# Attention with beacon keys and a low-rank mixer: values of the first batch loaded in long rows and held until the first q is there, first pair turned in two parts

## The chip, the cores and the metric

The kernel runs on one core of a Trainium2 chip. A core has engines that work side by side, each on its own list of instructions in order: TensorE (PE: matmuls and transposes, with PEld for its weight loads), VectorE (DVE), ScalarE (ACT), GpSimd (POOL) and SyncE (SP). Transfers are issued from the lists of SP, ACT and POOL. The metric is the time of one execution in microseconds on the device.

## The reference

Eight batches, eight heads, 576 tokens, head size 64. Sixteen "beacon" keys and values stand ahead of each head's 576; they are seen by all tokens. The attention's output, with the heads side by side (512 wide), goes through a mixer of rank 32 over the tokens and then through an MLP 512 to 2048 to 512 with a residual.

```python
k_all = concatenate([beacon_k, k], axis=2)          # 16 + 576
v_all = concatenate([beacon_v, v], axis=2)
scores = q @ k_all.T / sqrt(64)                     # causal, beacons always seen
a = softmax(scores)
x = (a @ v_all).transpose(0, 2, 1, 3).reshape(8, 576, 512)
u = x + (x.transpose(0, 2, 1) @ U @ V).transpose(0, 2, 1)
out = u + maximum(u @ w_ch1, 0) @ w_ch2
```

## The kernel before

**Tiles.** Two heads make a pair; there are 32, four to a batch. For each pair k and q are turned (head size on partitions), scores are computed transposed (keys on partitions) in four visits a to d for both heads, each visit followed by two exponentials on ACT out of PSUM into `expt`. DVE masks by a minimum, PE multiplies with the values (`po`), DVE divides by the sum that a column of ones gives, into `xb`. When a batch's four pairs are done the mixer forms `uT`, a ring of three blocks of 512 tokens. The MLP runs over nine such blocks: 16 products `g` a block for the hidden layer, then seven products of a two-by-two scheme with sums on DVE (`p`, `W`, `P`).

**The order.** `SCRIPT` is a list of steps, written out; every engine's list is in the script's order. A step's name gives engine and pair where it matters: V is DVE, A is ACT, G is POOL. `GkV1` casts or regroups pair 1's k on DVE (`regroup`, L294). `HqA0` casts pair 0's short q rows ("heads", the first 64 or 80 rows, `first_heads`, L791) on ACT. `TkA1` turns pair 1's k on PE and copies it out on ACT (`qkT_units`, L302 to L308). `Sb2:1` is visit b of pair 2 with one filler matmul (`keep_warm`, L282); `I1` is one filler alone. `M0.1` and `A0.1` are mask and value product of pair 0, head 1. `X0.0` to `X0.2` are the mixer of batch 0, whose last two write `uT`. `g0.5` is a hidden product of block 0, `R12` a turn of a pair by a transfer. `k1A`, `q1B`, `v0A`, `b1` and `w10` are loads, with A and B the halves of four heads.

**The first batch.** Its q and k come in f32 over SP's and ACT's lists (`load_first`), pair by pair, into `stm` (512 main rows) and `sth` (heads). All other loads are issued by POOL and cast to f16 on the way. A main row of q or k is four tokens in a row of DRAM, 1,024 bytes of f32.

**Values.** `v_loads` (L212) fetches them in five loads for a half batch, one token and head (64 numbers) a piece, straight into `vs`, where partitions are tokens. For a batch in `PACKED`, `packed_loads` (L220) fetches 448 of the 576 tokens four at a time into a tile `xt` and the rest as before; the step `O` (`unpack`, L231) then brings them to `vs` by 16 matmuls with a 0/1 matrix `unp` (filled by the step `n`) and four copies out of PSUM, two on DVE and two on ACT. Before, only batch 1 is packed.

**Buffers.** PSUM tiles come from one pool of eight buffers in turn, so a matmul waits until the tile eight before is copied out. `hold`, the step `Y` (L793), lets POOL copy one number of a loaded tile; what stands behind it on POOL is issued only when that tile has landed. No step `Y` stood in the script before.

Of the kernel before, what the change touches and what calls it, by code (L numbers as in the profile page):

```python
# [27 lines left out]
def kernel(  # L28
# [267 lines left out]
    def qkT_units(L, pr, qT, kT, c, copies):  # L296

        hs = ds(2 * c, 2)

        def one(i, dst, w):  # L300
            ps = pst([P, SK], F16, name="tps")
            nc.tensor.transpose(ps[:, 0:NL], L[0][i][:NL, hs, :], ident[:NL, :NL])  # L302
            for j in range(4):
                nc.tensor.transpose(ps[:, ds(NL + P * j, P)], pr[:, i, j, :, :], ident)  # L304
            copies[i](out=dst[:, c, 0 : w - 4 * P], in_=ps[:, 0 : w - 4 * P])
            copies[i](
                out=dst[:, c, w - 4 * P : w].rearrange("x (p j) -> x p j", j=4),
                in_=ps[:, NL:SK].rearrange("x (j p) -> x p j", j=4),  # L308
            )
# [529 lines left out]
    def step(t):  # L839
# [75 lines left out]
        v1B b2 M5.0 g0.8 GqV7 GqV6 TkA6 TkA7 M4.1 g0.10 M4.0 U0.1 TqA7 w13 TqA6 A5.0 GqA9 A5.1 GqV8 A4.1
        A4.0 Sd7 Sc7 g0.2 Sd6 Sc6 Sb6 g0.7 g0.3 k2 O1B g0.6 GqV10 Sb7 Sa6:0 Sa7 p00.0 w20 M6.0 g0.12 g0.13
        p00.1 GkV8 w21 v2 M7.1 GkV9 GkA10 g0.15 M7.0 TqA8 A6.0 TqA10 M6.1 p00.2 TkA9 A7.0 A7.1 TkA8 TqV9
        A6.1 g0.14 g0.4 Sb8 Sc8 Sd8 X1.0 p01.0 TkV10 P01.0 X1.2 Sa8 GqV11 p01.1 P01.1 GkV11 b3 X1.1 W0 Sb9
        P02.0 Sd9 Sc9 Sa9 W4 W1 W5 M8.0 W2 W6 TqA11 M8.1 TkA11 b4 P02.1 U1.1 M9.1 p01.2 M9.0 P05.0 U0.3
        P05.1 P06.0 q3 P06.1 A9.1 k3 A8.1 A8.0 W3 A9.0 P03.0 q4 P03.1 Sb11 Sa11 g1.10 GqV14 GqV13 k4 g1.7  # L920
        g1.2 GkA13 P07.0 Sb10 Sc11 Sd11 GkA12 GkV14 g1.15 g1.1 GqV12 g1.3 R12 M11.0 R13 R14 g1.12 g1.9 g1.8
        g1.14 g1.4 Sc10 Sd10 Sa10 W7 M11.1 P07.1 M10.1 b5 g1.5 U1.0 A11.1 g1.6 U1.3 A10.1 TkV13 TkV12 TqA13
        g1.0 P04.0 g1.13 M10.0 v3 TqV12 GqV16 P04.1 A10.0 GkV15 g1.11 GkV17 p11.0 TkV14 A11.0 p10.0 U1.2
        Sb12 Sc12 Sc13 P11.0 P11.1 GqA15 R15 X2.0 p11.1 Sa12 Sd12 Sa13 p10.1 M12.1 P16.0 p10.2 M12.0 X2.1
        p11.2 TqA14 q5 P12.0 P12.1 GkV16 A12.0 GqA17 R16 A12.1 P16.1 U2.2 P15.0 R17 Sd13 Sb13 Sc14 x12
        P15.1 TkV15 P17.0 P17.1 Z16 M13.1 Sa14 Sd14 TqA15 Sb14 U2.3 P13.0 M13.0 P13.1 GkA19 g2.11 TkA16
        M14.1 A13.1 v4 A13.0 P14.0 M14.0 TqA16 P14.1 Sa15 Sb15 Sd15 A14.0 GqV19 A14.1 g2.14 Sc15 Sb16 Sc16
        GkV18 M15.0 M15.1 GqV20 TqV17 g2.2 TkA17 g2.13 A15.0 A15.1 g2.9 N5 g2.0 x14 Sd16 Sa17 Sd17 g2.7
        g2.6 X2.2 X3.0 Sb17 Sc17 N1 Sa16 x13 g2.8 k5 M17.0 GqV18 U2.0 M16.0 g2.3 x15 M17.1 g2.10 b6 R18 R19
        U2.1 g2.1 g2.15 GkV20 M16.1 A16.0 A17.1 X3.2 R20 Z18 q6 g2.4 b7 p20.0 g2.5 p20.1 g2.12 A16.1 GkA21  # L930
        P21.0 p21.0 X3.1 P21.1 TkA18 P22.0 TqA18 GqV21 GkV22 TqA19 P22.1 p21.1 TkA19 A17.0 p21.2 Sb18 Sc18
        p20.2 P26.0 P26.1 GkV23 Sd18 k6 GqV22 Sa19 Sa18 M18.0 P25.0 P25.1 M18.1 P27.0 GqA23 Sb19 Sd19 Sc19
        TqA20 P23.0 R21 U3.0 M19.0 M19.1 P27.1 x16 GqA24 P23.1 TkA20 TqV21 v5 g3.1 g3.11 A18.1 g3.9 R22
        A19.0 A19.1 TkV21 g3.3 g3.14 g3.13 Sd21 Sb21 Sc21 R23 P24.0 g3.12 A18.0 q7 g3.5 P24.1 Sb20 U3.3
        U3.1 Sd20 g3.10 Sa21 Sa20 Sc20 X4.0 g3.6 GkV24 M21.0 M21.1 g3.8 M20.0 g3.7 TkA22 M20.1 TqV23 g3.15
        g3.2 x17 g3.4 GkV25 g3.0 A21.1 R24 x18 p31.0 TkA23 p31.2 A21.0 P31.0 Sa23 Sc23 Sb23 TqA22 p30.0
        GqA25 U3.2 P31.1 P32.0 A20.0 A20.1 p30.2 x19 R25 P32.1 GqA26 Sd23 Sc22 P36.0 GkV26 Sa22 Sb22 Sd22
        p30.1 GkV27 p31.1 GqA28 R26 M23.1 TkV24 GqA29 GqA27 k7 M22.0 P36.1 P35.0 X4.1 TqA25 A23.1 P35.1
        P37.0 P37.1 X4.2 A22.0 TqA24 U4.1 P33.0 TkA26 P33.1 g4.1 M23.0 v6 GkA29 GkA28 g4.2 M22.1 g4.12 R27
        N6 N2 TqA26 g4.7 g4.11 R28 g4.3 g4.14 TkA25 g4.15 A22.1 Sc24 Sa24 A23.0 g4.10 P34.0 v7 Sb25 Sb24  # L940
        Sd24 g4.5 R29 g4.6 P34.1 TqV27 Sc25 Sa25 Sd25 M24.1 M25.0 M25.1 TkA27 g4.4 g4.8 g4.13 M24.0 U4.3
        A25.0 g4.0 A25.1 Sd27 Sc27 Sb27 X5.0 p41.0 A24.0 x21 p41.1 g4.9 A24.1 Sa27 Sa26 Sc26 p40.0 M27.0
        P41.0 p40.1 GqV31 P42.0 A27.0 M27.1 U4.2 GkA30 U4.0 x22 Sb26 p41.2 GkV31 x23 Sd26 p40.2 P45.0 M26.1
        P45.1 x20 A27.1 P41.1 P42.1 TqA29 TkV28 M26.0 TqA28 P43.0 X5.1 GqA30 U5.3 R30 P46.0 A26.1 P46.1
        P43.1 g5.12 U5.1 x27 g5.4 TkV29 g5.2 g5.5 N3 N7 g5.0 Sa29 Sd29 Sc29 P47.0 P47.1 A26.0 Sb29 Sd28
        M29.0 M29.1 Sb28 P44.0 g5.3 g5.1 R31 x24 A29.0 P44.1 X5.2 g5.6 g5.15 Sa28 Sc28 TqV31 A29.1 TqV30
        TkV31 M28.0 x25 g5.7 U5.0 N4 g5.10 M28.1 TkV30 g5.9 Sa31 Sb31 Sd31 A28.0 g5.8 A28.1 g5.11 X6.0 Sd30
        x29 x26 Sc31 X6.1 V6.0 g5.14 p50.0 M31.1 p50.1 g5.13 p51.0 p51.1 Sa30 Sb30 Sc30 P51.0 M31.0 A31.1
        M30.1 P51.1 P55.0 M30.0 x28 P52.0 A31.0 A30.1 p50.2 U5.2 P56.0 U6.1 A30.0 p51.2 V6.1 P56.1 x31
        P55.1 P52.1 X7.0 X6.2 P57.0 x30 N0 P57.1 F61.0 P53.0 X7.1 V6.2 P53.1 U6.2 P54.0 F66.0 X7.2 F65.0  # L950
        F61.1 F62.0 F67.0 F62.1 P54.1 U7.2 F63.0 F61.2 F65.1 F66.1 V6.3 F65.3 F62.2 F61.3 F65.2 F67.1 F62.3
        V7.2 U7.0 U7.3 F64.0 V7.0 F66.2 U7.1 F63.1 V7.1 U6.3 F66.3 F63.2 F75.0 F71.3 F71.0 F64.1 F67.3
        F76.3 p60.0 F67.2 F63.3 p61.0 F64.3 P61.0 p60.1 F64.2 F75.3 p61.1 p60.2 V8.0 U6.0 P61.1 P62.0 P65.0
        P65.1 V7.3 F76.0 P66.0 p61.2 P62.1 P63.0 P66.1 P63.1 F72.3 F77.3 F77.0 F75.2 F72.0 F75.1 F73.3
        F73.0 F71.2 P67.0 F71.1 F74.3 F72.2 F76.1 V8.2 F76.2 F81.0 F72.1 P67.1 F77.1 F77.2 F73.2 P64.0
        P64.1 p71.0 U8.2 F74.0 p71.1 F73.1 F74.1 P71.0 F81.1 p70.0 F85.3 p70.1 F74.2 P71.1 P72.0 P72.1
        P76.0 V8.1 P75.0 p71.2 p70.2 P75.1 P76.1 guard F86.1 V8.3 P73.0 F86.0 P73.1 F85.1 U8.1 P77.0 P77.1
        F82.0 F85.0 F82.1 F87.1 F87.0 F83.0 F83.1 F81.2 U8.0 F84.1 P74.0 F81.3 P74.1 p80.0 F86.2 F82.3
        p80.1 F86.3 F82.2 F85.2 F84.0 F87.2 F87.3 F83.2 F83.3 sum p81.0 F84.2 F84.3 P81.0 P81.1 U8.3 p81.1
# [122 lines left out]
```

## Time and profile before

| | us |
|---|---|
| median of three timed executions | 338.77 |
| the three | 339.65, 336.57, 338.77 |
| the profiled execution's own time | 336.31 |
| its span, first to last instruction | 334.6 |

The profile shows one execution, with the TensorE clock granted at 0.999 of full speed. Its span leaves out 1.7 us that lie around it. A row of the timeline gives the start, the time from the first start to the last end, the engine, the line, the operation with what it writes and reads, and a count. An instruction's time overlaps with that of the one behind it on the same engine, so spacings of starts are shorter than the durations. Square brackets tell how long the engine stood idle in front and what ended it. The chain of waits gives start, length and work, with no overlap.

Some rows that set the scene, from the timeline: what PE does until the first pair is in, and where it waits in the first 30 us.

```profile
1.58 4.88 PE L282 MATMUL idle<-ident 128*128 128x512 f16 x11 [1.58 <-POOL ident masks.py:199]
...
8.21 0.68 PE L357 MATMUL sps<-qT,kT 64*128 64x336 f16 x10 [0.35 <-DVE small L158]
...
15.48 1.21 PE L357 MATMUL sps<-qT,kT 64*128 64x208 f16 x10 [0.40 <-ACT kT L109]
...
23.69 0.63 PE L372 MATMUL po<-vs,expt 128*128 128x65 f16 x15 [0.61 <-DVE expt L345]
```

### The profile page before, as it was taken

To read this page: it belongs to the slowest core of one execution; us is meant where nothing else is said; L and a number is where in the kernel's file an instruction comes from. 1 tells how busy PE (TensorE), PEld (TensorE's weight loads), DVE (VectorE), ACT (ScalarE), POOL (GpSimd) and SP (SyncE) were. 2 spreads that over 40 slices of the span, in tenths; PEclk is the share of its full clock that TensorE was granted. 3 is DMA by queue.
4 is the path that set the end of the run, shared out by engine and by line. 5 is a ranking of instruction groups with operands and counts; after the bars stand their busy time and mean duration, and the time that the engine had idled before them with its cause. 6 is when DMAs were issued, how large, how long until landed. Compare 5 with 4: busy or idle time off the path is not lost.

```text
span 334.6 us, 8971 instructions
## 1 busy us (share of the span) xinstructions
PE 324.8 (97%) x3537; PEld 227.2 (68%) x3537; DVE 257.8 (77%) x684; ACT 232.0 (69%) x510; POOL 96.6 (29%) x125
## 2 busy tenths in 40 slices
...
GB/s 186 222 201 167 156 198 193 119 189 213 118 164 162 203 149 143 143 131 177 191 121 143 183 168 112 31 169 123 68 41 80 141 19 63 3 80 94 80 37 99
DMA packets 133393, 44.18 MB, mean 132 GB/s; under 512 B 104768, under 2 KB 129216, under 8 KB 133344
## 3 DMA queue, kind: packets, MB, share of 16 engines
...
q14 instruction: 20, 0.16, 0.2%
...
## 4 chain that ended last, share of the span: by engine, by line
PE 87%; DVE 5%; ACT 4%; DMA 2%; issue 1%; SPq 0%
PE gps L570 25%; PE cpY L661 19%; PE cpD L661 9%; PE sps L357 8%; PE po L372 7%; PE fpY L607 6%; PE cpA L661 4%; PE fpD L607 3%; ACT expt L362 3%; PE fpA L607 2%; DMA stm<-in_k_dram 1%; PE ups L438 1%; PE ups L431 1%; PE qtp L412 1%; PE tps L304 1%; DVE ob L686 1%
## 5 line engine op out<-in xcount | busy, mean ns | idle before, releaser
L362 ACT ACTIVATE expt<-sps 128x496 f16<-128x496 f32 (+2 forms) x256 | 110.5, 576 | 13.3 <-PE sps L357 7.5
L570 PE MATMUL gps<-uT,w 128*128 128x512 f16 x384 | 90.2, 379 | 0.2 <-DVE xb L381 0.2
L570 PEld LDWEIGHTS <-w 128*128 128x128 f16 x384 | 34.9, 98 | 39.5 <-issue 2.6
L661 PEld LDWEIGHTS <-gT 128*128 128x128 f16 x576 | 54.7, 98 | 9.4 <-issue 1.5
L628 POOL TENSOR_SCALAR gT<-gT 128x512 f16<-128x512 f16 x12 | 18.3, 1534 | 103.9 <-DVE gT L622 70.9
L661 PEld LDWEIGHTS <-sT 128*128 128x128 f16 x432 | 40.7, 98 | 6.9 <-issue 0.7
L575 DVE SCALAR_TENSOR_TENSOR gT<-gps,gT 128x256 f16<-128x256 f32 x48 | 19.7, 420 | 29.7 <-ACT gT L574 29.5
L372 PEld LDWEIGHTS <-expt 128*128 128x128 f16 (+1 forms) x960 | 34.4, 98 | 7.2 <-issue 1.3
L580 ACT ACTIVATE gT<-gps 128x512 f16<-128x512 f32 x48 | 29.9, 637 | 12.7 <-PE gps L570 12.7
L372 PE MATMUL po<-vs,expt 128*128 128x65 f16 (+1 forms) x960 | 37.1, 194 | 0.6 <-DVE expt L345 0.6
L661 PE MATMUL cpD<-w,sT 128*128 128x256 f16 x288 | 36.1, 273 | 0.0
L661 PE MATMUL cpY<-wsum,gT 128*128 128x256 f16 x288 | 36.1, 273 | 0.0
L357 PE MATMUL sps<-qT,kT 64*128 64x80 f16 (+4 forms) x384 | 34.0, 281 | 1.5 <-ACT kT L109 0.4
L381 DVE TENSOR_TENSOR xb<-po,rec 128x320 f16<-128x320 f32 x64 | 31.5, 491 | 2.2
L212 POOL DMA_DIRECT2D vs<-in_v_dram x40 | 32.6, 833 | 0.8 <-DMA hd<-in_k_dram 0.8
L109 ACT ACTIVATE hP<-fpY 128x512 f32<-128x512 f32 x24 | 14.0, 596 | 26.8 <-PE fpY L607 16.6
L345 DVE TENSOR_TENSOR expt<-expt,bigmask 128x512 f16<-128x512 f16 x64 | 26.7, 417 | 6.6 <-ACT expt L362 6.6
L574 ACT ACTIVATE gT<-gps 128x256 f16<-128x256 f32 x48 | 19.8, 440 | 12.3 <-PE gps L570 12.2
L357 PEld LDWEIGHTS <-kT 64*128 64x128 f16 x384 | 14.8, 94 | 19.2 <-issue 11.0
L686 DVE TENSOR_TENSOR ob<-cpY,ut 128x512 f32<-128x512 f32 (+1 forms) x28 | 18.6, 665 | 2.6 <-PE cpY L661 2.4
L607 PEld LDWEIGHTS <-wf 128*128 128x128 f16 x192 | 18.6, 98 | 2.6 <-DVE tb L549 0.2
L661 PE MATMUL cpY<-w,gT 128*128 128x256 f16 x144 | 18.4, 273 | 0.0
(123 smaller groups left out, 480.8 us busy)
## 6 DMA issues: line engine op xcount, KB each, us to landing
...
```

The source lines that it names most:

```text
L212: nc.gpsimd.dma_start(out=dst[a : a + nq[j], j, :, :], in_=src[hs, ds(q0[j], nq[j]), :].rearrange("h p d -> p h d"))
L345: nc.vector.tensor_tensor(out=e4, in0=e4, in1=bigmask, op=ALU.min)
L357: nc.tensor.matmul(ps[i][:, ds(o, w)], kT[hp, c, ds(P * ch, P)], qT[hp, c, ds(qa, w)], start=True, stop=True,)
L362: nc.scalar.activation(out=ex[i][:, ds(PAD + SLOT * g, gw[g])], in_=ps[i][:, 0 : gw[g]], func=AF.Exp, scale=scale)
L372: nc.tensor.matmul(po[:, j, :], ex[0 : nk[c], ds(blk[(c, j)], P)], vs[0 : nk[c], ds(c * H * E + h * E, E)], start=(c == 0), stop=(c == j),)
L381: nc.vector.tensor_tensor(out=xb[:, h // 2, :, ds(D * (h % 2), D)], in0=po[:, :, 0:D], in1=r.broadcast_to([P, NT, D]), op=ALU.mult)
L570: nc.tensor.matmul(g, w1[:, cc, ts(dc, P)], uT[:, cc, ds(ring(t0), 512)], start=(cc == 0), stop=(cc == NCC - 1))
L574: nc.scalar.activation(out=gT[:, dc, 0:H2], in_=g[:, 0:H2], func=AF.Relu)
L580: nc.scalar.activation(out=gT[:, dc, :], in_=g, func=AF.Relu)
L607: nc.tensor.matmul(ps[:, i, :], a[:, kk, ts(2 * mp + i, P)], b[:, kk, :], start=opens and i == 0 and kk == 0, stop=kk == 1, skip_group_che ...
L661: nc.tensor.matmul(ps[:, i, :], a[:, f, ds(P * i, P)], b[:, f, :], start=opens and i == 0 and f == 0, stop=f == NK - 1, skip_group_check=True,
L686: nc.vector.tensor_tensor(out=out, in0=ps[:, ii, :], in1=other, op=ALU.add)
```

## The change

Batch 0 is packed too, so its values come in eight loads instead of twelve and need two unpacks, `O0A` and `O0B`. A step `Yq0` stands in the script ahead of all loads on POOL: it holds them until the main rows of pair 0's q have landed. A new function turns a pair's main rows and its heads as two steps, `j` and `l`, each with a PSUM tile of its own; pair 0 uses them. And the script of some 940 steps is another, but for its last 324 (from `Sd27` on): which engine casts and copies what, the place of the loads, of `O1A` (now ahead of the mixer of batch 0) and of the later steps. Seven steps `I1` are gone.

```diff
-    PACKED = (1,)
+    PACKED = (0, 1)
...
+    def turn_part(L, pr, dst, c, i, main, copy):
+        w = (SK, S)[i]
+        ps = pst([P, SK], F16, name="tps")
+        if main:
+            for j in range(4):
+                nc.tensor.transpose(ps[:, ds(P * j, P)], pr[:, i, j, :, :], ident)
+            copy(
+                out=dst[:, c, w - 4 * P : w].rearrange("x (p j) -> x p j", j=4),
+                in_=ps[:, 0 : 4 * P].rearrange("x (j p) -> x p j", j=4),
+            )
+        else:
+            nc.tensor.transpose(ps[:, 0:NL], L[0][i][:NL, ds(2 * c, 2), :], ident[:NL, :NL])
+            copy(out=dst[:, c, 0 : w - 4 * P], in_=ps[:, 0 : w - 4 * P])
...
+        elif name in "jl":
+            b, c = divmod(int(arg[2:]), NH2)
+            i = "kq".index(arg[0])
+            turn_part(Ls[b], prs[int(arg[2:])], (kTs[b % 2], qT_of(b))[i], c, i, name == "j", COPY[arg[1]])
...
-        I1 GqV0 I1 HkA0 I1 I1 B GkA0 I1 I1 I1 v0A GkV1 v0B I1 I1 HqA0 I1 I1 TkA0 TqV0 TkA1 u Sc0 Sd0 Sb0
...
+        Yq0 I1 I1 HqA0 GkV0 I1 n v0A I1 u v0B I1 q1A q1B s I1 I1 GqV0 b1 I1 jkV0 HkV0 jqV0 lkA0 lqA0 B k1A
+        w10 GkV1 GqV1 Sb0 Sc0 TkV1 Sa0:3 TqV1 v1A GkV2 Sd0 Sd1 Sc1 M0.0 Sa1:2 M0.1 GqV2 O0A Sb1 w12 GkV3
...
```

POOL's list at its start, before: the value loads of both halves, then the first loads of batch 1 (`vs` are the values, `st` and `hd` main rows and heads of q and k).

```order
L759 MEMSET vs_128 128x40
L202 DMA vs_127<-in_beacon_v_dram 16x4x64
L212 DMA vs_127<-in_v_dram 112x4x64
L212 DMA vs_127<-in_v_dram 128x4x64 x3
L212 DMA vs_127<-in_v_dram 80x4x64
L202 DMA vs_127<-in_beacon_v_dram 16x4x64
L212 DMA vs_127<-in_v_dram 112x4x64
L212 DMA vs_127<-in_v_dram 128x4x64 x3
L212 DMA vs_127<-in_v_dram 80x4x64
L205 DMA st_296<-in_k_dram 128x4x256
```

The same place now, with the hold (`gate`) in front and `xt` as the tile of packed rows.

```order
L774 MEMSET vs_128 128x40
L810 COPY gate<-stm 1x1
L222 DMA xt<-in_v_dram 112x4x256
L202 DMA vs_127<-in_beacon_v_dram 16x4x64
L227 DMA vs_127<-in_v_dram 112x4x64
L227 DMA vs_127<-in_v_dram 16x4x64
L222 DMA xt<-in_v_dram 112x4x256
L202 DMA vs_127<-in_beacon_v_dram 16x4x64
L227 DMA vs_127<-in_v_dram 112x4x64
L227 DMA vs_127<-in_v_dram 16x4x64
L205 DMA st_209<-in_q_dram 128x4x256
```

Every load of POOL now stands behind the copy of one number of `stm`; behind the values comes batch 1's q, where its k came.

DVE's list behind its memsets, before: the first row is pair 0's q.

```order
L294 CAST pr<-stm 128x512
L118 MEMSET bigmask 128x16
L119 COPY bigmask<-mask 128x112
L121 COPY bigmask<-mask 128x128 x3
L294 CAST pr<-stm 128x512
L791 CAST hd_142<-sth 80x128
L305 COPY qT<-tps 128x64
L306 COPY qT<-tps 128x512
L158 MEMSET small 16x32
L294 CAST pr<-stm 128x512
```

And now: the second cast is pair 0's k, and the two copies at L320 are its turned main rows and q's.

```order
L294 CAST pr<-stm 128x512
L126 MEMSET unp 128x66
L127 TENSOR_REDUCE unp<-ident 128x32
L158 MEMSET small 16x32
L168 COPY one<-ident 32x32 x4
L294 CAST pr<-stm 128x512
L320 COPY kT_125<-tps 128x512
L806 CAST hd_142<-sth 80x128
L320 COPY qT<-tps 128x512
L118 MEMSET bigmask 128x16
L119 COPY bigmask<-mask 128x112
L121 COPY bigmask<-mask 128x128 x3
```

The fills of `unp` and `one` have moved up from behind pair 1, `bigmask` has moved back, pair 1's k is cast behind all of this, and pair 0's k is cast and copied here and no longer on ACT.

ACT's list at the later visits of pair 1 (`sps` are visits), before:

```order
L362 ACTIVATE expt_123<-sps_317 128x496
L362 ACTIVATE expt_124<-sps_318 128x496
L362 ACTIVATE expt_123<-sps_327 128x464
L362 ACTIVATE expt_124<-sps_328 128x464
L109 ACTIVATE kT_125<-tps 128x80
L109 ACTIVATE kT_125<-tps 128x512
L109 ACTIVATE kT_125<-tps 128x80
L109 ACTIVATE kT_125<-tps 128x512
```

The same place now (`vps` are unpacked values):

```order
L377 ACTIVATE expt_123<-sps_320 128x496
L377 ACTIVATE expt_124<-sps_321 128x496
L377 ACTIVATE expt_123<-sps_332 128x496
L377 ACTIVATE expt_124<-sps_333 128x496
L109 ACTIVATE vs_127<-vps 128x4x64
L109 ACTIVATE vs_127<-vps 64x4x64
L377 ACTIVATE expt_123<-sps_368 128x464
L377 ACTIVATE expt_124<-sps_369 128x464
L109 ACTIVATE kT_125<-tps 128x80
L109 ACTIVATE kT_125<-tps 128x512
```

The first unpack's two copies stand between visits a and b of pair 1, and one of the two turned k behind them has gone to DVE.

More of the change, by code (lines that the diff above doesn't have):

```diff
@@ L915 @@
[L915 to L959, printed above, removed]
@@ new lines @@
+        Sc12 Sb12 Sd13 GqV15 GkV15 TkA14 P11.1 P12.0 GqV16 P12.1 q5 R15 Sd12 TqA14 X2.0 Sa12 Sb13 Sc13
+        p11.2 GqV17 M12.1 GkA16 M12.0 P15.0 P16.0 p10.2 X2.1 P16.1 A12.1 R16 P15.1 U2.2 A12.0 P17.0 Sa13
+        Sd14 Sb14 M13.0 R17 M13.1 TkA16 P17.1 TqV15 TkV15 P13.0 x12 U2.3 P13.1 A13.1 GkV18 g2.9 A13.0 Sc14
+        Sa14 Sd15 P14.0 TqV16 M14.1 g2.1 g2.7 TkA17 Z16 Sa15 Sc15 Sb15 M14.0 P14.1 A14.0 v4 A14.1 g2.10
+        TqV17 M15.0 k5 x14 GkV19 b6 g2.5 GqV20 M15.1 Sc16 Sa16 Sb16 A15.0 g2.0 g2.2 A15.1 g2.8 X2.2 GqV18
@@ new lines @@
+        Sd16 X3.0 Sd17 M16.0 x13 U2.0 Sc17 Sb17 Sa17 A16.0 x15 GqA19 g2.6 M17.0 g2.15 g2.4 M16.1 g2.3 g2.11
+        g2.12 R18 P21.0 p20.0 p20.1 X3.2 GkV20 g2.13 R19 g2.14 U2.1 M17.1 A16.1 p21.0 GqV21 Z18 TkA18 X3.1
+        q6 A17.0 p21.1 GqV22 R20 P21.1 A17.1 TqA18 p20.2 TkA19 b7 P22.0 TqA19 P22.1 GkA21 R21 Sb18 GkV22
+        Sc19 P25.0 U3.0 p21.2 P26.0 k6 P26.1 Sb19 Sd19 Sa18 x16 P25.1 P27.0 P27.1 Sc18 Sa19 Sd18 P23.0 v5
+        P23.1 M19.0 TqA20 g3.4 g3.10 g3.15 M19.1 TkV21 TqV21 M18.1 g3.0 A19.0 R22 g3.1 GkV23 g3.2 A19.1
@@ new lines @@
+        A18.1 g3.6 GkA26 M18.0 g3.5 GqV23 Sa21 Sb21 g3.14 TkV20 A18.0 R23 g3.3 P24.0 Sd21 Sc21 Sd20 GqV26
+        P24.1 U3.3 M21.0 TqV22 GkV25 q7 g3.7 Sc20 Sb20 Sa20 TkV22 N1 g3.13 g3.9 M21.1 g3.11 U3.1 GkA24
+        M20.0 TkV23 g3.12 x17 TqV23 A21.0 A20.0 M20.1 GqA24 R24 p31.0 g3.8 A21.1 GqV25 Sc23 Sa23 Sb23 A20.1
+        x18 P31.0 p30.0 P31.1 Sd23 Sd22 X4.0 Sa22 U3.2 x19 p30.1 GkA27 p31.1 Sc22 Sb22 M23.0 p31.2 M23.1
+        R25 R26 P32.0 P36.0 P32.1 TkV24 TqA24 P35.0 p30.2 k7 P36.1 M22.0 X4.1 TkA25 GqA27 P35.1 P37.0 X4.2
@@ new lines @@
+        x20 A27.1 P41.1 P42.1 TqA29 TkV28 M26.0 TqA28 P43.0 X5.1 GqA30 U5.3 R30 P46.0 A26.1 P46.1 P43.1
+        g5.12 U5.1 x27 g5.4 TkV29 g5.2 g5.5 N3 N7 g5.0 Sa29 Sd29 Sc29 P47.0 P47.1 A26.0 Sb29 Sd28 M29.0
+        M29.1 Sb28 P44.0 g5.3 g5.1 R31 x24 A29.0 P44.1 X5.2 g5.6 g5.15 Sa28 Sc28 TqV31 A29.1 TqV30 TkV31
+        M28.0 x25 g5.7 U5.0 N4 g5.10 M28.1 TkV30 g5.9 Sa31 Sb31 Sd31 A28.0 g5.8 A28.1 g5.11 X6.0 Sd30 x29
+        x26 Sc31 X6.1 V6.0 g5.14 p50.0 M31.1 p50.1 g5.13 p51.0 p51.1 Sa30 Sb30 Sc30 P51.0 M31.0 A31.1 M30.1
```

34 lines of the change are left out of this document (29 added, 5 removed).

## The prediction

> **What bounds the kernel now.** I read the page's first lines, then the windows, the chain of waits, and last the timeline of each engine up to 35 us.
>
> ```profile
> span 334.6 us, 8971 instructions
> PE 324.8 (97%) x3537; PEld 227.2 (68%) x3537; DVE 257.8 (77%) x684; ACT 232.0 (69%) x510; POOL 96.6 (29%) x125
> ```
>
> ```profile
> core 0: us, PE busy (x) PEld busy (x) DVE busy (x) ACT busy (x) POOL busy (x), PEclk, DMA share, GB/s
> 10.00:15.00 5.00, 4.25 (x66) 2.76 (x64) 4.61 (x20) 5.00 (x13) 4.18 (x7) 1.00 1.66 217
> 20.00:25.00 5.00, 3.96 (x81) 3.00 (x77) 4.87 (x20) 5.00 (x15) 2.35 (x4) 1.00 1.35 201
> 25.00:30.00 5.00, 4.79 (x79) 2.84 (x76) 3.52 (x12) 3.94 (x11) 1.24 (x2) 1.00 1.49 192
> ...
> 30.40:55.00 24.60, 24.60 (x308) 13.93 (x311) 17.38 (x58) 24.16 (x65) 14.20 (x19) 1.00 1.50 175
> 55.00:72.00 17.00, 16.81 (x227) 12.83 (x228) 16.18 (x41) 10.73 (x28) 6.84 (x9) 1.00 2.32 153
> ```
>
> PE idles 9.8 us in all (334.6 less 324.8). The windows put its losses before 30 us: there ACT is busy without a break and DVE almost, and PE waits for both. From 30.4 us on PE is full. So the change, which alters every engine's work before 30 us, can win only there; an order after that can lose but hardly win.
>
> ```profile
> 8.63 6.18 ACT expt L362 x14
> 29.43 0.99 PE sps L357 x13
> 30.42 2.69 PE gps L570 x12
> 35.34 0.55 PE vps L240 x16
> 36.86 0.04 PE tps L302
> 36.90 0.22 PE tps L304 x4
> 52.65 1.73 PE gps L570 x8
> ```
>
> The chain has ACT's exponentials from 8.63 and PE's MLP products from 30.42. Those two marks frame the stage, so I work out where each lands after the change.
>
> **When the first exponential starts.** These are DVE's rows to 30 us that start after an idle time, and those that price its steps.
>
> ```profile
> 4.62 0.43 DVE L294 CAST pr<-stm 128x512 f16<-128x512 f32 x1 [2.97 <-DMA stm<-in_q_dram]
> 6.80 0.43 DVE L294 CAST pr<-stm 128x512 f16<-128x512 f32 x1 [1.30 <-DMA stm<-in_k_dram]
> 7.38 0.68 DVE L306 COPY qT<-tps 128x512 f16<-128x512 f16 x1
> 8.75 0.22 DVE L791 CAST hd<-sth 80x128 f16<-80x128 f32 x1 [0.27 <-DMA sth<-in_q_dram]
> 10.36 0.19 DVE L305 COPY qT<-tps 128x64 f16<-128x64 f16 x1 [1.38 <-PE tps L304]
> 11.06 0.42 DVE L294 CAST pr<-stm 128x512 f16<-128x512 f32 x1
> 11.39 0.41 DVE L791 CAST hd<-sth 80x128 f16<-80x128 f32 x1
> 12.01 0.57 DVE L168 COPY one<-ident 32x32 f16<-32x32 f16 x4
> 12.32 0.41 DVE L345 TENSOR_TENSOR expt<-expt,bigmask 128x512 f16<-128x512 f16 x1
> 16.55 0.42 DVE L345 TENSOR_TENSOR expt<-expt,bigmask 128x512 f16<-128x512 f16 x1 [0.37 <-ACT expt L362]
> 17.49 0.11 DVE L126 MEMSET unp<- 128x66 uint32 x1
> 17.64 0.38 DVE L127 TENSOR_REDUCE unp<-ident 128x32 f16<-128x128 f16 x1
> 27.84 0.72 DVE L447 CAST uT<-ups 128x240 f16<-128x240 f32 x2 [0.53 <-PE ups L438]
> 29.49 0.92 DVE L447 CAST uT<-ups 128x336 f16<-128x336 f32 x2 [0.93 <-PE ups L438]
> 36.37 0.75 DVE L244 CAST vs<-vps 128x256 f16<-128x256 f32 x2
> ```
>
> ```profile
> 5.70 0.61 ACT L109 ACTIVATE pr<-stm 128x512 f16<-128x512 f32 x1
> 6.22 0.29 ACT L109 ACTIVATE hd<-sth 80x128 f16<-80x128 f32 x1
> 6.88 0.72 ACT L109 ACTIVATE kT<-tps 128x80 f16<-128x80 f16 x2 [0.37 <-PE tps L304]
> ...
> 26.12 2.43 ACT L362 ACTIVATE expt<-sps 128x208 f16<-128x208 f32 x6 [0.68 <-PE sps L357]
> ...
> 29.45 0.79 ACT L449 ACTIVATE uT<-ups 128x336 f16<-128x336 f32 x2 [0.38 <-PE ups L438]
> 30.13 2.97 ACT L362 ACTIVATE expt<-sps 128x496 f16<-128x496 f32 x6
> 35.99 0.73 ACT L109 ACTIVATE vs<-vps 128x256 f16<-128x256 f32 x2
> ```
>
> Pair 0's q lands as before: DVE casts it at 4.62, and no value load competes with it in either order before then. The cast holds DVE 0.33 (11.06 to 11.39): 4.95. Then `unp` is filled, 0.53 (17.49 to 18.02): 5.48; four copies for `sel`, 0.31 (12.01 to 12.32): 5.8. k0's cast, which ACT began at 5.70, now follows on DVE: 6.13. From the end of that cast on ACT (6.31) to the copy of the turned rows (6.88) went 0.57, so the new main copy of k starts at 6.7; two such copies at 0.68 with a small head cast of 0.2 between end at 8.26. Before, the corresponding copy ended at 8.06 and the first exponential came 0.56 later. The new one is due at about 8.8, or 8.6 if the copies overlap their tails as before. I take 8.7: turning heads apart saves nothing, because DVE's list in front is full. Freeing the transfers from the value packets cannot help this mark, as k0 had landed before 5.70 already.
>
> **ACT to the last `uT` copy before the MLP.** Before: 8.63 to 30.13 is 21.5 us, less its idle 0.68 and 0.38 is 20.45 of work. Exponentials are the same 38, the turned copies for pairs 2 to 5 stay four. New are three unpacks (two for batch 0, and batch 1's first, now placed ahead of this mark) at 0.73, 2.2 us, and one head cast of 0.25 to 0.29 with q3. Sum 22.9; 8.7 and 22.9 make 31.6.
>
> **DVE to the same mark.** Before: 4.62 to 30.41, 25.8 us, less its idle (1.30, 0.27, 1.38, 0.37, 0.53, 0.93: 4.78) is 21.0. New: six casts of values (0.75 a pair), 2.25; seven full turned copies and two main ones for six full, 0.70 (10.36 to 11.06) and 1.36; two regroups more, at most 0.33 each. That is 5.0, so 26.0 and, begun at 4.62, 30.6 without any idle. The 0.57 behind k0's cast and about half of the last two waits remain, which makes 31.2 to 32.1. I take 31.6 for both engines.
>
> **PE.** The two added unpacks cost 2 x 0.55, the seven `idle` matmuls taken out are fillers; both lie in time in which PE waits, so they count nothing. That cover is PE's idle, 0.75 us between 10 and 15 and 1.04 between 20 and 25 in the windows above; were it gone, 1.1 us would show. The first MLP product moves from 30.42 to 31.6, 1.2 later. By then PE has done 0.55 (batch 1's unpack) and 0.26 (the turned q of pair 7) that came later before, and has still to do one visit of pair 4, 6 of 14 in 0.99, 0.42. So it is 1.2 - 0.39 = 0.8 us behind.
>
> **Loads.** The value loads wait for q0 on POOL, and all loads behind them too. The first row is POOL's first load in the timeline; the others are loads of the first 80 us in the view of transfers, with KB each and the us from issue to landing (unpacked values, then packed main rows).
>
> ```profile
> 2.30 0.72 POOL L202 DMA_DIRECT2D vs<-in_beacon_v_dram  x1
> ```
>
> ```profile
> vs<-in_v_dram POOLq DMA_DIRECT2D x6, 64.0 KB, 5.8
> ...
> xt<-in_v_dram POOLq DMA_DIRECT2D x2, 224.0 KB, 10.2
> ```
>
> Eight issues from about 4.8 at 0.72 end near 10.6, twelve from 2.30 near 10.9; what is queued behind keeps its time. Half A is wanted by its unpack at about 13. Bounds for its landing are 5.8 to 10.2 after the issue, 10.6 to 15.0; I take 12, nearest to the early loads, for 0 on the path. After 8.75 no idle time of DVE or ACT in the rows above ends with a transfer, so cheaper packets are worth 0. SP's queue keeps its order and stays free.
>
> **From 31 us on.** Engines, regroups and turned copies are dealt out anew up to about 225 us, in PE's full stage; I count 0. At most about 0.2 us of PE idle can be won there (17.00 less 16.81).
>
> [...]
>
> **Sum.** 336.31 (profiled execution) + 0.8 = 337.1. The four known executions run 336.31 to 339.65 with mean 337.8, and the median of the three timed is 2.46 above the profiled one. On the mean's scale the time is 338.6.
>
> **Rivals.**
>
> A, faster: DVE's waits at 6.80 to 10.36 (2.95) vanish and nothing takes their place, so both lists end at 30.6 to 30.9 with k0 turned early; then the first product is 0.2 to 0.4 late, less 0.39, and if the first exponential also starts 0.9 earlier, -0.9: 336.9. For it: those idle times are real. Against: ACT's 22.9 us cannot shrink. More than 1% (3.4 us) would take a third of all the idle time that PE has in the program.
>
> B, slower: the held values land late. If they land at 15.0, PE, which works in order, stands at the unpack, whose 0.55 end at 15.6. In front of it stand 14 exponentials, as in the chain's first row, some narrower: 8.7 and 6.18 make 14.9 at most, 14.4 with the narrow ones. ACT loses 1.0, for +1.8: 339.6. It decides from a landing at 14.1; for more than 1% slower it must land near 17. Against: the fewer packets. [...]
>
> C, slower: DVE becomes the bound between 55 and 72 us. It has 0.8 us of room (16.18 of 17.00), and between 31 and 57 us three turned copies and two regroups more are dealt to it, 2.6 us, which eat into its 7.2 us of room in 30.4 to 55. If none of that is worked off by 55, PE waits up to 2.6 for DVE there: with the forecast's 0.8, +3.4 at the far end, +1.8 if half of it stays: 339.6.
>
> D: the dealt-out order after 31 us wins or loses on its own by 1 to 3 us, as matmuls that start at other moments behind other weight loads; either sign, 335.6 to 341.6. [...]
>
> **How the numbers follow.** Forecast 0.60, its own range 337.2 to 339.9; A 0.16, B 0.09, C 0.09, D 0.06. A single median scatters by about 1.5 (336.57 to 339.65). One percent, 3.4 us, is about what a measurement can tell from no change. The range goes from A with its scatter and D's gain, 335.6, to C's far end with some scatter, 341.4. Faster by over 1%: parts of A and D with scatter, 0.10. Slower: the far ends of B and C and part of D, 0.11. Within: 0.79. No more than 2 in 10 lies outside the range.
>
> **What would show it.** Right: first exponential at 8.6 to 8.8; first MLP product at 31.2 to 32.1; ACT and DVE nearly full from 9 to 30 us; PE full behind it. Wrong: an exponential at 8.0 or earlier (A), PE or ACT idle at 13 to 16 us ended by a value load (B), PE idle ended by DVE at 55 to 75 us (C), a first MLP product below 30.5 or above 33.

## The result, and the profile after

| | before | after |
|---|---|---|
| median of six executions, us | 337.82 | 348.52 |
| the range of the six | 336.55 to 339.65 | 347.18 to 350.40 |
| the profiled execution: time, span | 336.31, 334.6 | 348.95, 347.3 |
| its mean granted clock | 0.999 | 0.984 |

The ratio is 1.0321, interval 1.0269 to 1.0373: slower by 3.2%, where no change was forecast. The prediction was wrong, and far outside its range.

One thing about the order was read wrongly ahead of the prediction: in the changed kernel DVE's first cast is pair 0's k (4.78, it waited for a load of k) and the second, at 5.99, is q. The text had them the other way round. It takes a term out of the sum for the first exponential, as said below.

First the page's head of the changed kernel, then its windows. The columns of a window are its bounds, its length, the busy time and count of PE, PEld, DVE, ACT and POOL, the granted clock, the DMA share and GB/s.

```profile
span 347.3 us, 9024 instructions
...
PE 328.3 (95%) x3562; PEld 228.0 (66%) x3562; DVE 267.1 (77%) x705; ACT 226.1 (65%) x497; POOL 94.7 (27%) x122
```

```profile
5.00:10.00 5.00, 2.96 (x26) 1.77 (x26) 4.59 (x23) 2.31 (x7) 4.72 (x6) 0.85 0.98 212
10.00:15.00 5.00, 4.32 (x41) 1.56 (x40) 3.25 (x12) 3.72 (x11) 4.70 (x8) 0.81 1.39 239
70.00:80.00 10.00, 7.35 (x47) 4.20 (x47) 5.81 (x15) 1.49 (x4) 0.00 (x0) 0.83 1.52 216
180.00:190.00 10.00, 7.96 (x93) 6.03 (x90) 8.17 (x20) 1.54 (x3) 5.27 (x7) 1.00 1.42 117
190.00:200.00 10.00, 7.54 (x42) 3.29 (x43) 1.81 (x6) 8.44 (x15) 0.00 (x0) 0.83 1.61 170
```

The same windows of the kernel before, behind the first stage:

```profile
70.00:80.00 10.00, 9.81 (x58) 4.49 (x57) 5.00 (x15) 8.64 (x20) 0.00 (x0) 1.00 1.47 214
180.00:190.00 10.00, 10.00 (x86) 5.69 (x83) 7.59 (x20) 7.22 (x14) 0.47 (x1) 1.00 1.94 177
190.00:200.00 10.00, 10.00 (x93) 5.35 (x90) 4.48 (x15) 9.62 (x24) 4.73 (x6) 1.00 1.96 163
```

The loss has three places. At the start the clock is 0.85 and 0.81 where it was 1.00. At 70 to 80 us and again at 180 to 200 us PE stands for some us, where it had been full, and the clock is at 0.83 in the slot with the end of the wait or behind it. In every other window of 10 us behind 30 us PE is busy at least 9.4 us in both. PE's timeline shows what ended the two large waits.

```profile
72.65 3.26 PE L676 MATMUL cpD<-w,sT 128*128 128x256 f16 x16 [2.97 <-DVE ob L701]
...
192.47 0.66 PE L372 MATMUL sps<-qT,kT 64*128 64x464 f16 x4 [4.51 <-ACT qT L109]
193.06 3.46 PE L585 MATMUL gps<-uT,w 128*128 128x512 f16 x8
```

Behind each wait the products ran at about half speed: 16 `cpD` in 3.26 behind the first, where 16 took 1.91 at 64.65, and eight `gps` in 3.46 behind the second, where PE's timeline of the kernel before has eight in 1.90 at 71.64. What the named engines themselves waited for is in their own timelines, DVE's first, then ACT's:

```profile
71.90 0.69 DVE L701 TENSOR_TENSOR ob<-cpD,ut 128x512 f32<-128x512 f32 x1 [3.76 <-issue]
```

```profile
189.88 1.06 ACT L109 ACTIVATE kT<-raw 128x512 f16<-128x512 f16 x1 [8.46 <-DMA raw<-pr]
```

The second is plain: ACT stood 8.46 us for `raw`, a pair turned by a transfer (step `R25`). The first names no cause, but the sum reads `ut`, the turned block `uT`, and the last of its transfers (step `U0.3`) was issued at 62.8 and took at most 9.0 us to land, which is 71.8. So both waits are for a turn, which is a transfer issued on SP. The views of the `ut` turns between 57 and 76 us, before and then after, give the duration on SP in ns, the starts, and the time to landing:

```profile
L561 SPq DMA_TRANSPOSE ut<-uT x2: 1190/1225/1260, 60.4 to 61.6; - x2
...
DMA to landing us min/median/max: 5.2/5.3/5.5
```

```profile
L576 SPq DMA_TRANSPOSE ut<-uT x2: 1189/2004/2818, 61.6 to 62.8; - x2
...
DMA to landing us min/median/max: 6.8/7.9/9.0
```

The two are the same two turns in the same order on SP. What differs is POOL's first large load of that place (batch 3's q). These are POOL's timelines, before and after:

```profile
62.62 0.89 POOL L205 DMA_DIRECT2D st<-in_q_dram  x1
```

```profile
61.34 0.90 POOL L205 DMA_DIRECT2D st<-in_q_dram  x1
```

Before, the first turn was on its way 2.2 us ahead of the loads and the second 1.0. Now the loads come 0.3 us ahead of the first, and both turns land late. Of the second turn's 3.8 us more (9.0 against 5.2), 1.6 us are spent on SP already, where its own instruction takes 2,818 ns in place of 1,260. At the second place it is the same: before, `R25` and `R26` went out ahead of batch 7's k, now behind it. The views of these turns and POOL's timeline, before and then after:

```profile
L324 SPq DMA_TRANSPOSE raw<-pr x2: 1231/1248/1265, 172.0 to 173.4; - x2
...
DMA to landing us min/median/max: 3.1/3.2/3.2
```

```profile
174.22 0.88 POOL L205 DMA_DIRECT2D st<-in_k_dram  x1 [22.06 <-DVE pr L294]
```

```profile
L339 SPq DMA_TRANSPOSE raw<-pr x2: 1252/2627/4002, 179.6 to 180.9; - x2
...
DMA to landing us min/median/max: 10.3/11.3/12.4
```

```profile
178.88 0.88 POOL L205 DMA_DIRECT2D st<-in_k_dram  x1 [15.63 <-ACT pr L109]
```

The brackets also show what lets the load go: POOL has been waiting, and a cast into `pr`, the reader of its buffer, ends that, once on DVE and once on ACT. Whether loads or SP's own list make the turns late is what the experiments test.

### The profile page after: what moved, and what is told of

Its sections match the earlier page's. It is cut to its first block, busy times and chain, and to the rows that moved or that the text cites. A ratio compares the mean times of both kernels' runs of the same rounds, so it can differ in the third digit from the quotient of the medians.

```text
span 347.3 us, 9024 instructions
## 1 busy us (share of the span) xinstructions
PE 328.3 (95%) x3562; PEld 228.0 (66%) x3562; DVE 267.1 (77%) x705; ACT 226.1 (65%) x497; POOL 94.7 (27%) x122
## 4 chain that ended last, share of the span: by engine, by line
PE 78%; ACT 9%; DVE 5%; DMA 4%; issue 2%; SPq 1%; DVEq 0%; ACTq 0%
PE gps L585 22%; PE cpY L676 16%; PE cpD L676 8%; PE po L387 7%; PE fpY L622 6%; PE sps L372 6%; ACT expt L377 4%; PE cpA L676 3%; PE fpD L622 3%; DMA raw<-pr 3%; ACT kT L109 2%; ACT qT L109 2%; PE fpA L622 2%; PE tps L304 1%; DMA stm<-in_k_dram 1%
## 5 line engine op out<-in xcount | busy, mean ns | idle before, releaser
L377 ACT ACTIVATE expt<-sps 128x496 f16<-128x496 f32 (+2 forms) x256 | 110.7, 546 | 10.1 <-PE sps L372 9.4
L585 PE MATMUL gps<-uT,w 128*128 128x512 f16 x384 | 92.6, 385 | 0.0
L676 PEld LDWEIGHTS <-sT 128*128 128x128 f16 x432 | 41.4, 99 | 10.3 <-issue 3.8
L387 PEld LDWEIGHTS <-expt 128*128 128x128 f16 (+1 forms) x960 | 35.2, 98 | 7.9 <-issue 0.9
L676 PE MATMUL cpD<-w,sT 128*128 128x256 f16 x288 | 37.4, 279 | 3.0 <-DVE ob L701 3.0
L595 ACT ACTIVATE gT<-gps 128x512 f16<-128x512 f32 x48 | 28.9, 624 | 15.6 <-PE gps L585 15.3
L387 PE MATMUL po<-vs,expt 128*128 128x65 f16 (+1 forms) x960 | 38.1, 194 | 0.0
L589 ACT ACTIVATE gT<-gps 128x256 f16<-128x256 f32 x48 | 19.0, 414 | 22.1 <-PE gps L585 21.9
L372 PEld LDWEIGHTS <-kT 64*128 64x128 f16 x384 | 13.8, 94 | 23.4 <-issue 11.5
L212 POOL DMA_DIRECT2D vs<-in_v_dram x30 | 25.8, 876 | 3.6 <-ACT qT L109 2.9
## 6 DMA issues: line engine op xcount, KB each, us to landing
st<-in_k_dram POOLq DMA_DIRECT2D x6, 512.0 KB, 10.5
```

What stands on the lines that cost most here:

```text
L212: nc.gpsimd.dma_start(out=dst[a : a + nq[j], j, :, :], in_=src[hs, ds(q0[j], nq[j]), :].rearrange("h p d -> p h d"))
L372: nc.tensor.matmul(ps[i][:, ds(o, w)], kT[hp, c, ds(P * ch, P)], qT[hp, c, ds(qa, w)], start=True, stop=True,)
L377: nc.scalar.activation(out=ex[i][:, ds(PAD + SLOT * g, gw[g])], in_=ps[i][:, 0 : gw[g]], func=AF.Exp, scale=scale)
L387: nc.tensor.matmul(po[:, j, :], ex[0 : nk[c], ds(blk[(c, j)], P)], vs[0 : nk[c], ds(c * H * E + h * E, E)], start=(c == 0), stop=(c == j),)
L585: nc.tensor.matmul(g, w1[:, cc, ts(dc, P)], uT[:, cc, ds(ring(t0), 512)], start=(cc == 0), stop=(cc == NCC - 1))
L595: nc.scalar.activation(out=gT[:, dc, :], in_=g, func=AF.Relu)
```

## The experiments

All kernels are the changed one with the edit shown, unless the text says otherwise. "First MLP product" is the start of the first `gps` in PE's timeline, and ratios are to the kernel before, timed beside it.

| kernel | median us | ratio, interval | first MLP product |
|---|---|---|---|
| fillers back at the start | 345.78 | 1.0283, 1.0213 to 1.0353 | 31.79 |
| U0.3 earlier | 342.98 | 1.0156, 1.0110 to 1.0203 | 31.71 |
| R25 earlier | 348.06 | 1.0266, 1.0201 to 1.0330 | 32.23 |
| these three together | 342.60 | 1.0140, 1.0072 to 1.0207 | 31.75 |
| changed start, order of before behind it | 343.92 | 1.0191, 1.0152 to 1.0229 | not compared |
| start of before, changed order behind it | 354.23 | 1.0507, 1.0457 to 1.0558 | not compared |
| loads held at both places | 338.98 | 1.0045, 1.0024 to 1.0066 | 30.74 |
| fillers in the second wait | 346.40 | 1.0259, 1.0227 to 1.0290 | 31.93 |
| U0.3 earlier, loads held at R25 | 338.02 | 1.0002, 0.9963 to 1.0041 | 31.91 |
| the same without the hold on q | 339.02 | 1.0036, 0.9986 to 1.0086 | 34.42 |
| the same with fillers at the start | 337.19 | 0.9986, 0.9942 to 1.0029 | 31.33 |
| the same without packing batch 0 | 339.88 | 1.0066, 1.0029 to 1.0102 | 32.35 |

### Fillers back at the start

```diff
-    jkV0 HkV0 jqV0 lkA0 lqA0 B
+    jkV0 HkV0 I4 jqV0 I2 lkA0 lqA0 I2 B
```

> The changed kernel with eight filler matmuls put back between the first pair's turned parts, where PE stood 0.99, 0.33 and 0.35 us; nothing else. Theory 1 (three places: a short list of fillers at the start, a late turn of uT at 69 us, a late turn of pair 25 at 188 us, each a wait and then some 9 us at a lower granted clock): clock 1.00 between 10 and 15 us where it was 0.81, first MLP product near 31.6 us (it was 32.7), time 1.0 to 1.5 us below the changed kernel, about +9.4 us against before. Rival 1 (the lists of ACT and DVE set that mark, the clock does nothing): mark stays at 32.5 to 33, time unchanged, +10.7.

The clock is 1.00 in both slots from 5 to 15 us, and ACT is full again in the second:

```profile
5.00:10.00 5.00, 4.71 (x44) 2.28 (x42) 4.41 (x22) 2.96 (x8) 5.00 (x8) 1.00 1.03 224
10.00:15.00 5.00, 4.13 (x75) 2.64 (x74) 4.67 (x17) 5.00 (x16) 3.50 (x6) 1.00 1.45 236
```

The first MLP product is at 31.79 in place of 32.72. The two late turns stay (waits of 1.40 and 3.51), so most of the loss is elsewhere. PE now also waits for packed values, 0.79 us at the second unpack of batch 0 and 1.30 at the first of batch 1, which the late start of the changed kernel had covered:

```profile
16.08 0.62 PE L240 MATMUL vps<-xt,unp 32*128 32x256 f16 x16 [0.79 <-DMA xt<-in_v_dram]
...
28.22 0.62 PE L240 MATMUL vps<-xt,unp 32*128 32x256 f16 x16 [1.30 <-DMA xt<-in_v_dram]
```

### The two late turns, each moved forward on SP

```diff
-    U1.1 W5 P01.0 P01.1 U0.3 W2
+    U1.1 W5 P01.0 P01.1 W2
...
-    U0.1 g0.1
+    U0.1 U0.3 g0.1
```

> The changed kernel with one step moved: U0.3, the last turn of block 0's uT by a transfer, right behind U0.1 (some 25 us earlier), no longer behind U1.1. Theory 1: PE's 2.97 us wait at 72.65 and DVE's 3.76 before it are gone and the granted clock between 70 and 80 us is 1.00 (it was 0.83); time 4 to 5 us below the changed kernel, about +6. Rival 2 (DVE was the bound in that stage, the turn only names the wait): PE waits as long for DVE at another step there, time within 1.5 us of the changed kernel.

```diff
-    R25 R26 P32.0
+    R26 P32.0
...
-    GqV25 Sc23
+    GqV25 R25 Sc23
```

> The changed kernel with one step moved: R25, the turn of pair 25 by a transfer, right behind the regroup of its q, ahead of two turns of x and one of uT on SP. Theory 1: PE's 4.51 us wait at 192.47 shrinks to under 1 us and the clock between 185 and 200 us is 1.00; time 5 to 6 us below the changed kernel, about +5. Rival 3 (the transfers of POOL make any turn late there, so the next turn takes its place): a wait of 3 us or more for another raw tile within 15 us, time within 2 us of the changed kernel.

`U0.3` earlier takes the first wait away, with the clock at 1.00 from 50 to 90 us, and the ratio falls from 1.0321 to 1.0156. `R25` earlier gains nothing that can be told from none. ACT no longer waits for `raw`, but the turn behind it is caught. PE's timeline, then the chain of waits at that place:

```profile
189.43 0.98 PE L387 MATMUL po<-vs,expt 128*128 128x65 f16 x15 [4.16 <-DVE uT L460]
```

```profile
179.33 9.54 DMA xt<-xb
```

An `xt` turn issued at 179.33 took 9.54 us, almost what `R25` took in its place (10.27 in the chain of the changed kernel). The slowness belongs to the moment, not to the turn.

### These three together

The edit is the three above at once.

> All three of the edits in one kernel. Theory 1: the gains add, 11 to 12 us; time -0.5 to +1 us against before, no PE idle of over 1 us behind 10 us. The forecast's +0.8 would then be the price of the packing and the hold. Rival 4 (the other order costs everywhere, waits hand over to each other): +4 us or more against before.

Start and first place are mended, but at the second place two turns still make waits of 1.78 and 1.14 (DVE stood 2.13 for a `ut` and 1.72 for an `xt`), with a clock of 0.66 in 180 to 190 us. What is left of the loss is 1.4%.

### Either half of the order alone

The first takes the changed kernel up to the mixer of batch 0 and then the open steps in the old order; the second, the other way round.

> The changed kernel up to the mixer of batch 0 (packing, hold, parted turns, its first steps and its order there), and behind that the steps still open in the order of the kernel before. Theory 1: the late turns come from the changed order behind 31 us. Then no wait of TensorE above 1 us at 65 to 80 and at 170 to 200 us, clock full there, and the time is 339 to 341, the cost of the start alone. Rival: the order behind 31 us is innocent, and a start that is 1 to 2 us late pushes the turns behind the loads whatever the order: then waits of 2 us and more stand there again and the time is 344 or more.

> The other half alone: the kernel before up to the mixer of batch 0 (values of batch 0 unpacked, no hold), and behind that the steps still open in the changed order. Theory 1 (the changed order behind 31 us costs by itself): 343 to 348, with the wait for kT of pair 25 at 180 to 190 us as in the changed kernel. Rival (only a late start tips it): 336.5 to 339, no wait above 1 us behind 60 us.

Both joints cost something of their own, which neither theory had: some loads stand elsewhere than in either kernel. In the first, PE waits 3.39 for a weight load at 38 us; in the second 3.46 for a load of q at 33 us:

```profile
38.38 6.18 PE L585 MATMUL gps<-uT,w 128*128 128x512 f16 x20 [3.39 <-DMA w<-in_moe_w_ch_dram]
```

```profile
33.30 0.25 PE L302 MATMUL tps<-ident,hd 80*128 80x80 f16 x1 [3.46 <-DMA hd<-in_q_dram]
```

So their times do not split the loss between the halves. Their turns still say something. With the old order PE has no wait above 0.5 us behind 60 us, although it comes to that place about 7 us late (turns at 67.9 in place of 60.4). A late start alone does not bring the late turns. With the changed order, on the old start, the wait at the first place is back and larger, while that at the second place is 1.69:

```profile
79.15 3.57 PE L661 MATMUL cpD<-w,sT 128*128 128x256 f16 x16 [4.10 <-DVE ob L686]
```

### Loads held at both places

The order stays, but POOL copies one number of the turned tile before it goes on, so that q3 to k4 wait for `U0.3`, and k7 and v6 wait for `R25`.

```diff
             if "u" not in cell:
                 cell["u"] = utp.tile([P, 4, DM], F16, name="ut", tag="ut")
+            if cc == 9:
+                nc.gpsimd.tensor_copy(out=gate2, in_=cell["u"][0:1, 0, 3 * P : 3 * P + 1])
+                return
...
-    M8.1 q3 A9.1
+    M8.1 U0.9 q3 A9.1
...
-    p30.2 k7 P36.1
+    p30.2 Z25 k7 P36.1
```

> The changed kernel with its order, but two one-number copies more on POOL: its loads q3, k3, q4, k4 wait until turn U0.3 has landed, and its loads k7, v6 until turn R25 has landed. Theory 2: the two turns are late because POOL's loads are under way with them. Then U0.3 takes under 4 us, R25 under 5 us, both waits of TensorE (2.97 and 4.51) fall below 1 us, and the time is 339 to 342. Rival (SP's own list, with several turns in a row, makes them late): both waits stay above 2 us, 346 to 350. Second rival: the held loads are late themselves, new waits for k3, q4 or k7 show behind them and the time stays above 344.

This gives nearly all of the loss back: 1.0045, from 1.0321, with no turn moved on SP. The hold itself in POOL's timeline, and the `ut` turns:

```profile
65.74 0.39 POOL L577 COPY gate<-ut 1x1 f16<-1x1 f16 x1 [5.13 <-DMA ut<-uT]
66.24 0.90 POOL L205 DMA_DIRECT2D st<-in_q_dram  x1
```

```profile
L579 SPq DMA_TRANSPOSE ut<-uT x2: 1191/1228/1265, 59.6 to 60.9; - x2
...
DMA to landing us min/median/max: 4.8/5.3/5.8
```

Both waits of PE are gone and the clock is 1.00 in every slot behind the start. The second rival is there too, but small: k3, held as well, lands 11.0 us after its issue at 67.85 (chain of waits), and PE stands 1.73 at 80.76.

The `ut` turns of all kernels in which the two stand together, in the order of the lead of the turns over POOL's first large load. Each line is read as the views above.

| kernel | first turn | first large load | lead | landing, us | wait of PE |
|---|---|---|---|---|---|
| loads held | 59.6 | 66.24 | +6.6 | 4.8 to 5.8 | none |
| before | 60.4 | 62.62 | +2.2 | 5.2 to 5.5 | none |
| changed start, old order | 67.9 | 70.08 | +2.2 | 2.5 to 2.9 | none |
| fillers back at the start | 60.7 | 61.69 | +1.0 | 5.8 to 7.4 | 1.40 |
| changed kernel | 61.6 | 61.34 | -0.3 | 6.8 to 9.0 | 2.97 |
| fillers in the second wait | 60.8 | 60.29 | -0.5 | 9.3 to 10.5 | 4.46 |
| R25 earlier | 61.1 | 60.50 | -0.6 | 8.3 to 8.9 | 2.95 |
| old start, changed order | 67.0 | 64.60 | -2.4 | 10.0 to 10.2 | 4.10 |

The landing follows the lead almost row by row. A turn that was on its way first landed in 2.5 to 5.8 us; one issued into the loads needed 6.8 to 10.5. Turns and loads come from two queues here, SP's and POOL's; in what order the single packets of the two went, no run shows.

### Fillers in the second wait

```diff
-    P33.1 g4.14 Sb25
+    P33.1 g4.14 I20 Sb25
```

> The changed kernel with 20 filler matmuls in front of visit b of pair 25, where TensorE stood 4.51 us. Theory 3 (the lower clock of 0.83 behind the wait comes from TensorE standing still): the clock at 190 to 200 us is 1.00, the wait goes into fillers, and the time falls by 1 to 2 us to about 347. Rival (the clock falls for another reason, or fillers do not count as work): clock at 190 to 200 us below 0.9 again and no gain, 348 to 350.

The wait stays, as 4.48 us of fillers and 0.82 of standing, but the products behind it run at full clock:

```profile
189.50 4.48 PE L282 MATMUL idle<-ident 128*128 128x512 f16 x20
...
194.80 0.58 PE L372 MATMUL sps<-qT,kT 64*128 64x464 f16 x4 [0.82 <-ACT qT L109]
195.32 1.90 PE L585 MATMUL gps<-uT,w 128*128 128x512 f16 x8
```

Eight `gps` take 1.90 in place of 3.46, 1.6 us less, and the ratio is 1.0259 in place of 1.0321, though the ends of the two intervals overlap. So at this place the low clock behind the wait came from PE standing still: the slot of 190 to 200 us has 1.00 with the fillers, 0.83 without. In this execution the first wait, without fillers, was 4.46 and the clock of that slot 0.66.

### U0.3 earlier and loads held at R25, and what is then left of the change

```diff
-    U0.1 g0.1
+    U0.1 U0.3 g0.1
...
-    p30.2 k7 P36.1
+    p30.2 Z25 k7 P36.1
```

> The changed kernel with turn U0.3 placed right behind U0.1 (as tried before) and POOL's loads k7, v6 held until turn R25 has landed (as tried before), but q3 to k4 not held. Theory 2 (each late turn came from loads under way beside it, and one of the two ways is enough for each): no wait of TensorE above 1 us at 60 to 90 us nor at 170 to 200 us, clock full, 335.5 to 338. Rival (moving one turn makes another late): a wait of 1.5 us or more there, 339 to 343.

The ratio is 1.0002. The waits at the two places are gone, but for 0.72 and 0.83 at 190 to 192 us, for DVE. This kernel and "U0.3 earlier" differ in the one copy `Z25` alone, and their views of `R25` and `R26` are the plainest rows of the study. Without the copy k7 is issued at 172.90, just ahead of the turns; with it at 179.37, behind them.

```profile
L339 SPq DMA_TRANSPOSE raw<-pr x2: 1265/3044/4822, 173.8 to 175.1; - x2
...
DMA to landing us min/median/max: 10.1/11.1/12.0
```

```profile
L339 SPq DMA_TRANSPOSE raw<-pr x2: 1253/1288/1323, 174.2 to 175.5; - x2
...
DMA to landing us min/median/max: 4.0/4.2/4.5
```

The same two turns at almost the same moment land in 4.0 to 4.5 in place of 10.1 to 12.0. That is worth the step from 1.0156 to 1.0002. SP's own list, the rival named for `U0.3`, can be left out here too: in both kernels four turns stand back to back on it right ahead of `R25`, from 168.4 and from 168.9 on.

On this kernel, where the rest is out of the way, the parts of the start were taken off one at a time.

```diff
-    Yq0 I1 I1 HqA0 GkV0
+    I1 I1 HqA0 GkV0
```

> As the kernel with U0.3 moved and k7, v6 held, but without the hold on pair 0's q at the start. Theory as predicted (the hold is worth 0, because q0 and k0 land before the values matter): first exponential within 0.3 us of the one with the hold, no wait for values at the first unpack, time within 1 us of it. Rival (the hold keeps the first loads free): q0 lands 0.5 us or more later, and the time is 1 to 2 us more.

```diff
-    jkV0 HkV0 jqV0 lkA0 lqA0 B
+    jkV0 HkV0 I4 jqV0 I2 lkA0 lqA0 I2 B
```

> As the kernel with U0.3 moved and k7, v6 held, with eight fillers put back among the turns of the first pair. Theory 4 (fillers there keep the clock up, which is otherwise low in some executions at 5 to 15 us): clock 1.00 from 5 to 20 us, the runs scatter less, the median 0.5 to 1.5 us below that without fillers. Rival (fillers are in the way of the turns): 0.5 to 1 us more.

```diff
-    PACKED = (0, 1)
+    PACKED = (1,)
...
-    GqV2 O0A Sb1
+    GqV2 Sb1
...
-    M1.0 O0B Sd2
+    M1.0 Sd2
```

> As the kernel with U0.3 moved and k7, v6 held, but the values of batch 0 not packed (twelve loads, no unpack for batch 0); the hold stays. Theory (packing pays for the hold: fewer issues, two unpacks of 0.55 on TensorE and 2.25 on DVE and 1.46 on ACT more): without it the values land later behind the hold, the first value products wait 1 us or more, 1 to 3 us slower. Rival (packing costs more than it brings): 1 to 2 us faster.

Without the hold the first exponential starts at 7.74, with it at 7.59, and no unpack of batch 0 shows a wait for values in either profile. The median is 1.0 higher, but the intervals of the two ratios overlap, and the one profile had a clock of 0.50 in 10 to 15 us, so what the hold is worth stays open between nothing and about 1 us. With the fillers the median is 0.8 lower, the clock is 1.00 from 5 to 20 us, and again the intervals overlap. The scatter is no smaller: nine of ten executions lie within 336.63 to 339.45 and one at 342.49, against 335.85 to 339.26 without fillers. This version stands level with the kernel before (0.9986, 0.9942 to 1.0029) and no other did better. Without packing PE waits for values again, and the median is 1.9 higher:

```profile
16.07 0.65 PE L387 MATMUL po<-vs,expt 80*128 80x65 f16 x16 [1.12 <-DMA vs<-in_v_dram]
```

Packing thus seems worth some 2 us as long as the hold stands in front of the loads; the ends of the two intervals (0.9963 to 1.0041, 1.0029 to 1.0102) just overlap.

## Why the prediction was wrong, point by point

**The order behind 31 us.** This is the step that failed: "From 31 us on … I count 0", and with it "SP's queue keeps its order and stays free". The order of the turns on SP was kept indeed, but not the order between SP's turns and POOL's loads. Nothing in the program ties the two together. The changed order brought the loads of q3 to k4 from 62.6 to 61.3 and the turns from 60.4 to 61.6, and at the second place k7, which had followed `R25` by 2.2 us, came 0.7 us ahead of it (178.88 and 179.59). The two fixes lower the ratio by 0.0319 in all, so that the whole loss, about 10.7 us, hangs on these two places. The two waits make 7.5 us (2.97 and 4.51). The clock behind the second costs at least 1.6 us on eight products (3.46 against 1.90). A slot of 10 us at 0.83 stands for about 1.7 us of lost clock (10 x 0.17), and there is one at each place, so waits and clock make an estimated 10.9 us. The prediction said itself that an order behind 30 us "can lose but hardly win", and still counted 0: a full PE bounds the gain, and the losses that rivals C and D priced had other causes.

**Rival C** named the place, 55 to 75 us, and the engine that PE would wait for, but not the cause. DVE was busy 5.81 of 10 us at 70 to 80 and stood 3.76 itself, for a transfer. **Rival D** is where this case belongs, a dealt-out order that loses, but its 1 to 3 us were the author's estimate for matmuls behind other weight loads, an effect that no run shows. One late turn already cost over 5 us (348.52 against 342.98 with `U0.3` earlier), and no transfer was priced there.

**The first MLP product** was forecast at 31.6 (31.2 to 32.1). In the changed kernel's profile it is at 32.72:

```profile
32.72 2.75 PE gps L585 x12
```

The words that may have failed are that the fillers taken out "count nothing". The sums for ACT and DVE were about right: in the kernels with this start and a full clock to 15 us the mark lies at 30.74 to 31.93, but for the one without packing. The clock was not in the sum. In nine profiles of this start without fillers, counting the one without packing and the one without the hold, it was below 0.9 somewhere from 5 to 15 us in five (marks from 31.91 up, where compared); in three with fillers it was full. That speaks for the fillers and does not prove it, since four executions had a full clock without them. In the medians the effect is too small to be told.

**The first exponential** was forecast at 8.6 to 8.8 and started at 8.35, and at 7.59 to 8.32 in the eleven other kernels with this start or most of it. Rival A's sign, 8.0 or earlier, stands in eight of them, although the first product came ahead of its range in one alone (30.74). The term that was too high is the 0.57 between the second cast and the copy of turned rows. The cast of k comes first, PE turns it while DVE casts q, and the copy starts as that cast ends. DVE's timeline of the changed kernel:

```profile
5.99 0.60 DVE L294 CAST pr<-stm 128x512 f16<-128x512 f32 x1
6.51 0.67 DVE L320 COPY kT<-tps 128x512 f16<-128x512 f16 x1
7.11 0.20 DVE L806 CAST hd<-sth 80x128 f16<-80x128 f32 x1
7.24 0.67 DVE L320 COPY qT<-tps 128x512 f16<-128x512 f16 x1
```

**ACT and DVE nearly full from 9 to 30 us** held only with a full clock. In the changed kernel's profile they have 3.72 and 3.25 of 5 us in 10 to 15.

**The loads and the hold**, counted 0. No wait for values shows in the changed kernel, whose start was late. In three of the six packed kernels with a full clock there is a wait of 0.25 to 0.79 at the second unpack of batch 0, none at the first, which rival B priced. Its mechanism is real and small. That no value load competed with pair 0's q in the order before was misread, since value loads went out from 2.30 on there, but without the hold k's cast started at 4.30, with it at 4.19. The hold's own worth stayed open.

**The net of the start**, +0.8, cannot be refuted: with both places mended the ratio is 1.0002 (0.9963 to 1.0041), and +0.8 is a ratio of 1.0024.
